# Scaled relus of ten tiles on VectorE, gates of three blocks by copies and gathers, one first load from ScalarE's queue, and a new order, in a gated linear-attention block

## The chip, the cores and the metric

The kernel runs on one core of a Trainium2 chip. The metric is the device time of one execution in microseconds (us), the median of several runs. In the profile PE is TensorE, ACT is ScalarE, DVE is VectorE, POOL is GpSimd, SP is SyncE, whose queue issues most of the DMAs; PEld is the loading of weights into TensorE.

## The reference

All data is float32: `x` is 2048 rows (tokens) of 512, H = 32 heads of 16.

```python
xn = layernorm(x)
# A: linear attention
q, k, v = heads(xn @ wqkv)                       # wqkv: 512 x 1536
phi = lambda t: where(t > 0, t + 1, exp(t)) + 1e-6
kv  = phi(k)^T v  per head;   z = sum over tokens of phi(k)
s   = (phi(q) kv) / (phi(q) . z + 1e-6) @ wo
# B: token mixing by shifts, then an MLP
h  = gelu(layernorm(xn) @ w1)                    # quarters shifted by +1, -1, +2, -2 tokens
x1 = xn + shifted(h) @ w2
y  = x1 + gelu(layernorm(x1) @ w3) @ w4          # w3: 512 x 1376
out = x + s * silu(y)
```

## The kernel before

**Tiles and stages.** The tokens are 16 tiles of 128 rows (`i` = 0 to 15), four tiles (`QT`) to a block `b` (0 to 3). Float32 accuracy is made of pairs: an operand is split into a rounded part and the rest (`hi`, `lo`), and a product is three matmuls (`products`). Products of 512 columns write a whole PSUM bank; there are four banks for running results ("mm") and four for long sums ("acc").

The first half of the program goes over the blocks. `load_u(b)` brings the block's transposed input `xt` and splits it into `u` (`ut` and `UT` in the code), `load_rows` brings `x` by rows and takes mean and variance: by two passes of ScalarE (tile `sq`) in block 0, by VectorE's statistics later; `scale_x` turns the variance into 1/sqrt on GpSimd (`rs`, `ns`, `nm`) and normalises the rows (`x`, `xh`, `xl`). For each tile there are then:

- `key(i)`: 12 matmuls into bank `k`; `feature_k` makes phi of it. `kt` = bank minus mean times column sum (VectorE), `kr` = relu(rs * kt) and then `kt` = exp(rs * kt) (ScalarE), `kr` = min(kt, 1) + kr (VectorE), then the halves `kh` and `kl`; a gather adds `kr` into `zacc`.
- `query(i)`: 12 matmuls into bank `q`; `qt` on VectorE, `qe` = relu(-rs * qt) and `qr` = relu(rs * qt) on ScalarE in another order of columns, `qe` = exp(-qe); `qr` is stored to memory and `qe` added there by a gather.
- `gram(i)`: 12 matmuls of `kh`, `kl` with `xh`, `xl` into the four long sums `g`.

`qneg` and `wneg` are the negated column sums of the weights; they come from one fp32 product each (`qsum`, `ksum`) with the sum of the four weight chunks (`wqt`, `wkt`). In the same half `mixer(b)` and `mix2(i)` do the token mixing (banks `h`, `pbm`, `pam`, `pem`). Between the halves `kv` and `m` join values and `wo`.

The second half goes over the blocks again. `up_last` (bank `a`) and five `up_pair`s (banks `pb`, `pa`, `pe`, a seven-product scheme, `seven`) make the MLP's hidden rows with gelu (`f`, `gf`); `down` adds their products with `w4` into the block's four accumulators (`acc`); `attend_pair` (banks `pbs`, `pas`, `pes`) makes `so`, the attention's output. In `seven` the bank `pb` is read by `p1` and `u2` on ScalarE and the bank `pe` by `p5`, before the next products go on top of them. `gate(i, a)` ends a tile: x1 is added to the accumulator, then tanh, two multiplications with `so`, a gather that adds `x`, and the store. The argument `late` chooses how x1 (kept in memory, `x1d`) is added: with it, x1 is fetched ahead and VectorE adds the accumulator; without it, ScalarE copies the accumulator and a gather of GpSimd adds x1 in SBUF. All calls of `before` use `late=True`. Blocks 0 to 2 call `gate` four times in a row; the last block has a code path of its own.

**The order.** The code above only records operations (`Plan.add`). `Plan.emit` then places them, engine by engine: it gives each a due time worked back from the order of TensorE's matmuls, keeps its own estimates of durations and of when an engine, a buffer or a DMA queue is free, and always takes the operation that can start first, by due time among those that can start within `slack`. TensorE may run ahead of its recorded order (`window`, `ahead`). Constants steer it: `PATIENCE` (how long a PSUM result may wait), `SAFE` (spare time behind a DMA), `lead` (how early buffers of a kind may be taken), and the table `SOONER`: pairs of an operation's number and how much earlier (in quarters of a us) it is due. The resulting order is fixed in the program; each engine works through its own list in order, and waits on semaphores.

`Plan.load` can issue a load from SP's queue or, with `eng="ACT"`, from ScalarE's; in `before` every load goes to SP. The first loads are the two halves of chunk 0 of block 0's `xt` (in `load_u`, parts > 1), and the key weights `wk_s`.

Of the kernel before, what the change touches and what calls it, by code (L numbers as in the profile page):

```python
# [10 lines left out]
AF = mybir.ActivationFunctionType  # L11
ALU = mybir.AluOpType
# [73 lines left out]
class Plan:  # L86
# [138 lines left out]


    GAP = .06
    PATIENCE = 2.5
    COLD, COLD_TILL = 1.84, 5.8
    SAFE = 2.0  # L230
    early = 0.0
    patience = 18.0

# [33 lines left out]
    def emit(self, first, lead, reserve, window, ahead, table=()):  # L267
# [20 lines left out]
        while left:  # L288
# [5 lines left out]
            for e, cands in avail.items():  # L294
                picks = []
                low = INF
                for op in cands:
                    s = max(free[e], op.ready)
                    if op.mb:
                        s = max(s, under[e == "POOL"][0] + self.GAP)  # L300
                    if op.two and s < port:
                        s = port
                    if e == "POOL" and not op.mb and not op.two:
                        s = next((b + .02 for a, b in lock if a <= s < b), s)
                    if op.table is not None and op.table != table:
                        s = max(s, free[e] + 1.28)
                    ok = True
                    fresh = [t for t in op.tiles if t.ap is None]
                    for t in fresh:
                        if t.tag not in slots:  # L310
                            continue
                        q = slots[t.tag]
                        need = sum(1 for u in fresh if u.tag == t.tag)
                        if len(q) < need:
                            ok = False
                            break
                        s = max(s, q[need - 1][0] + self.GAP)
                        if e == "PE":
                            if op is not front and (len(q) < 2 or op.nom - front.nom > ahead):
                                ok = False  # L320
                                break
                        elif t.tag in lead:
                            n = lead[t.tag] * (1.5 if len(q) > reserve[t.tag] else 1)
                            s = max(s, op.due + slip - n - t.early)
                    if not ok:
                        continue
                    if e == "PE" and op.nom - front.nom > window:
                        continue
                    q = s
                    if op.table is not None and op.table != table and op.due + slip < s:  # L330
                        q = s - 1.28
                    picks.append((q, s, op))
                    low = min(low, q)
                if not picks:
                    continue
                slack = .02 if e == "PE" else 0.08
                s, op = min(((s, op) for q, s, op in picks if q <= low + slack), key=lambda x: (x[1].due, x[1].order))
                if best is None or s < best[0]:
                    best = (s, op)
# [3 lines left out]
            e = op.eng  # L343
# [50 lines left out]
def linear_attn_gated_by_mixer(  # L394
# [20 lines left out]
    QT = 4  # L415
# [112 lines left out]
    def col(t, i):  # L528
        return t[:, i:i + 1]
# [105 lines left out]
    def load_u(b, parts):  # L635
# [3 lines left out]
        for q in range(parts):  # L639
            o = q * n  # L640
            for c in range(NC):
# [5 lines left out]
                        rounded(*(t[:, 2:2 + BT] for t in UT[b][c]), XT[b, c])  # L647
                    continue
                src = XT[b, c].cols(o, o + n)
                pl.load(src, xt[b, c][:, o:o + n])  # L650
                hi, lo = (t[:, 2 + o:2 + o + n] for t in UT[b][c])
                if b == q == 0 and parts > 1:
                    pl.ts(hi, src, 1.0, None, ALU.mult)
# [41 lines left out]
    def by_block(v):  # L695

        return v.via(lambda ap: ap.rearrange("p (b c k) -> p c b k", b=P // RB, k=RB))
# [41 lines left out]
    def feature_k(i, ps):  # L739

        t, r = piece(f"kt{i}"), piece(f"kr{i}")
        pl.stt(t, wneg, mean(mv1, i), ps, ALU.mult, ALU.add)
        pl.act(r, t, AF.Relu, scale=col(rs1, i))
        pl.act(t, t, AF.Exp, scale=col(rs1, i))
        hi, lo = rounds(f"k{i}")
        pl.stt(r, t, 1.0, r, ALU.min, ALU.add)
# [18 lines left out]
    def query(i):  # L765
# [2 lines left out]
        t, e, r = (piece(f"q{n}{i}") for n in "ter")  # L768
        pl.stt(t, qneg, mean(mv1, i), ps, ALU.mult, ALU.add)
        pl.act(by_block(e), by_chunk(t), AF.Relu, scale=col(ns1, i))  # L770
        pl.act(by_block(r), by_chunk(t), AF.Relu, scale=col(rs1, i))
        pl.act(e, e, AF.Exp, scale=-1.0)
        pl.soon(pl.store(pqd[i].all, r))
        pl.soon(pl.gather(pqd[i].all, e))
# [559 lines left out]
    for b in range(NQ):  # L1334
# [39 lines left out]
        if not last:  # L1374
# [2 lines left out]
                for j in range(QT):  # L1377
                    down(b, f, j, A[j])
            for j in range(QT):
                gate(b * QT + j, A[j], late=True)  # L1380
        else:
            i, (a, o) = b * QT + QT - 1, B[-1]
            XL[i] = piece(f"xo{i}")
# [15 lines left out]
                gate(b * QT + QT - 1, a, o, D // 2, late=True, by_dma=False, whole=o > 0)  # L1399

    SOONER = (
# [6 lines left out]
    )  # L1408
    pl.emit(first=6.0, lead={"p": 14.0, "w": 14.0, "ab": 10.0}, reserve={"p": 20, "w": 1, "ab": 0}, window=12.0,
            ahead=6.0, table=SOONER)  # L1410


# [35 lines left out]
```

## Time and profile before

| | |
|---|---|
| median of 3 runs | 519.17 us (518.96 to 519.18) |
| the profiled execution | 519.35 us, its span 517.6 us |
| PE busy | 511.2 us (99%), 3005 matmuls |
| DVE busy | 394.0 us (76%) |
| ACT busy | 324.8 us (63%) |
| POOL busy | 102.8 us (20%) |
| granted TensorE clock | 0.998 |

The span runs from the first instruction of the program to the last; the time has 1.75 us more around it. Busy time of PE is a union of modelled matmul spans that overlap, so a matmul that starts a little late need not show as idle time; the distance from one start to the next does show it. In rows of a timeline the columns are: start, duration, engine, line, operation, output and inputs (numbers left out), count, and in brackets the idle time of the engine ahead of it with what ended it. In rows of the chain: start, duration, what. In rows of a table by stretches: the stretch, its length, then busy us and instructions (x) of PE, PEld, DVE, ACT, POOL, then granted clock, DMA share and GB/s. In rows of groups: busy us, mean ns of one, and idle time before them.

### The profile page before, as it was taken

How to read it: one execution, taken by the hardware profiler on the slowest of the kernel's cores; microseconds unless marked ns; L12 is line 12 of the kernel's file. 1: busy time of each engine (PE TensorE's matmuls, PEld its weight loads, DVE VectorE, ACT ScalarE, POOL GpSimd, SP SyncE). 2: the span in 40 equal slices, each digit the busy share in tenths (PEclk: the TensorE clock that was granted, in tenths of full speed). 3: DMA queues.
4: the chain of work that ended last, by engine and by line, in shares of the span. 5: the costliest groups of instructions: out<-in, count | busy, mean ns of one | idle time of the engine just before them, and what ended most of it. 6: DMA issues, size and time to landing. Idle time of an engine off the chain costs nothing.

```text
span 517.6 us, 8927 instructions
## 1 busy us (share of the span) xinstructions
PE 511.2 (99%) x3005; PEld 445.0 (86%) x3005; DVE 394.0 (76%) x788; ACT 324.8 (63%) x664; POOL 102.8 (20%) x195
## 2 busy tenths in 40 slices
PE   8999999999999999999999999999999999999996
PEld 6777888988888888898889989899898898999985
DVE  5884987569567838999999999655886657895635
ACT  5899784579558657787866755345453545535621
POOL 1378643431363022211100001000020000200000
PEclk9999999999999999999999999999999999999999
DMA  8759994375976389989767759648488376687604
GB/s 277 255 101 248 225 205 97 74 172 182 220 169 162 68 185 249 259 261 262 287 200 225 237 175 249 212 152 208 133 214 276 122 201 157 179 248 225 243 1 122
DMA packets 73281, 100.12 MB, mean 193 GB/s; under 512 B 7844, under 2 KB 30900, under 8 KB 73236
## 3 DMA queue, kind: packets, MB, share of 16 engines
q1 hardware_dynamic: 63876, 82.52, 50.6%
q0 software_dynamic: 9360, 17.04, 19.9%
q8 instruction: 23, 0.38, 0.3%
q14 instruction: 22, 0.18, 0.1%
HBM read 60.33 MB, written 30.81 MB: 176 GB/s over the span
## 4 chain that ended last, share of the span: by engine, by line
PE 91%; ACT 5%; DVE 2%; DMA 1%; issue 1%; SPq 0%; DVEq 0%
PE acc L146 22%; PE pb L146 10%; PE k L146 8%; PE h L146 8%; PE q L146 7%; PE g L146 7%; PE pe L146 5%; PE pbs L146 5%; PE pbm L146 4%; PE pa L146 3%; PE pes L146 2%; PE a L146 2%; PE pem L146 2%; PE pas L146 1%; ACT y L167 1%; PE pam L146 1%
## 5 line engine op out<-in xcount | busy, mean ns | idle before, releaser
L223 POOL DMA_DIRECT2D th<-in_x x14 | 12.2, 919 | 247.3 <-PE a L146 126.2
L167 ACT ACTIVATE p<-pb 128x256 f32<-128x256 f32 x20 | 7.7, 385 | 25.8 <-PE pb L146 25.4
L223 POOL DMA_DIRECT2D o<-x x16 | 15.0, 935 | 40.4 <-DVE o L189 19.7
L223 POOL DMA_DIRECT2D zacc<-kr x16 | 14.6, 910 | 41.8 <-DVE kr L199 33.6
L167 ACT ACTIVATE th<-xo 128x512 f32<-128x512 f32 (+1 forms) x16 | 9.7, 619 | 19.3 <-DVE xo L189 16.2
L167 ACT ACTIVATE gf<-gf 128x512 f32<-128x512 f32 (+1 forms) x40 | 20.9, 523 | 0.8
L223 POOL DMA_DIRECT2D pqd<-qe x16 | 14.7, 921 | 28.9 <-ACT p5m L167 10.0
L167 ACT ACTIVATE p<-pe 128x256 f32<-128x256 f32 x20 | 7.7, 386 | 18.9 <-PE pe L146 18.9
L189 DVE TENSOR_TENSOR xo<-acc,xo 128x512 f32<-128x512 f32 (+1 forms) x16 | 10.3, 670 | 11.4 <-PE acc L146 11.4
L199 DVE SCALAR_TENSOR_TENSOR kt<-wneg,mv,k 128x512 f32<-128x512 f32 x16 | 11.9, 742 | 9.4 <-PE k L146 8.5
L199 DVE SCALAR_TENSOR_TENSOR kr<-kt,kr 128x512 f32<-128x512 f32 x16 | 11.0, 690 | 10.4 <-ACT kt L167 10.4
L199 DVE SCALAR_TENSOR_TENSOR qt<-qneg,mv,q 128x512 f32<-128x512 f32 x16 | 11.9, 742 | 7.2 <-PE q L146 7.1
L167 ACT ACTIVATE ht<-ht 128x512 f32<-128x512 f32 x16 | 10.0, 630 | 11.5 <-DVE ht L189 11.4
L189 DVE TENSOR_TENSOR gf<-u,pe 128x256 f32<-128x256 f32 x20 | 8.3, 416 | 11.2 <-PE pe L146 11.2
L189 DVE TENSOR_TENSOR gf<-pa,p 128x256 f32<-128x256 f32 x20 | 8.4, 418 | 10.5 <-PE pa L146 10.4
L189 DVE TENSOR_TENSOR ht<-h,abc 128x512 f32<-128x512 f32 x16 | 10.8, 686 | 6.5 <-PE h L146 6.5
L167 ACT ACTIVATE x<-x,nm,rs 128x512 f32<-128x512 f32 x16 | 12.5, 802 | 2.9 <-POOL nm L189 2.9
L167 ACT ACTIVATE qr<-qt,rs 128x512 f32<-128x512 f32 x16 | 11.4, 715 | 4.1 <-DVE qt L199 4.1
L590 DVE BATCH_NORM_STATS2 st<-o 128x6 f32<-128x512 f32 x16 | 10.9, 683 | 1.8 <-DMA o<-x 1.8
L167 ACT ACTIVATE kr<-kt,rs 128x512 f32<-128x512 f32 x16 | 11.4, 715 | 1.2 <-DVE kt L199 1.1
L167 ACT ACTIVATE y<-o,nm,rs 128x512 f32<-128x512 f32 x16 | 12.0, 805 | 0.1
L167 ACT ACTIVATE kt<-kt,rs 128x512 f32<-128x512 f32 x16 | 11.4, 715 | 0.1
(1559 smaller groups left out, 2195.9 us busy)
## 6 DMA issues: line engine op xcount, KB each, us to landing
w_s<-in_w SPq DMA_DIRECT2D x28, 256.0 KB, 5.5
x<-in_x SPq DMA_DIRECT2D x16, 256.0 KB, 5.2
zacc<-kr POOLq DMA_DIRECT2D x16, 256.0 KB, 3.9
pqd<-qr SPq DMA_DIRECT2D x16, 256.0 KB, 3.3
pqd<-qe POOLq DMA_DIRECT2D x16, 256.0 KB, 5.4
o<-x POOLq DMA_DIRECT2D x16, 256.0 KB, 4.6
x1d<-o SPq DMA_DIRECT2D x16, 256.0 KB, 4.9
pq<-pqd SPq DMA_DIRECT2D x16, 256.0 KB, 6.0
```

The costliest lines, as they stand in the source:

```text
L146: lambda: nc.tensor.matmul(out.get(), lhs.get(), rhs.get(), start=start, stop=stop, skip_group_check=more))
L167: nc.scalar.activation(out.get(), src.get(), func, scale=get(scale), **kw)
L189: self.vec(eng, out, [a, b], lambda: self.e(eng).tensor_tensor(out.get(), a.get(), b.get(), op=op), True)
L199: lambda: self.nc.vector.scalar_tensor_tensor(out.get(), a.get(), get(s), b.get(), op0=op0, op1=op1),
L223: lambda: self.nc.gpsimd.dma_start(out.get(), get(src), accum_op=ALU.add), mb=mb)
L590: pl.add("DVE", .62, .69, [xv], [st], lambda: nc.vector.bn_stats(st.get(), xv.get()))
```

## The change

Four things change, and the order of all engines with them.

1. The first half of `xt` (block 0, chunk 0) is issued by ScalarE's queue, so SP begins with the first key weight.
2. In `feature_k` the scaled relu of tiles 4 to 7 is one operation of VectorE (multiply by `rs`, then max with 0) instead of one of ScalarE; in `query` the same holds for `qr` of tiles 2 to 7. That is ten operations.
3. The gates of blocks 0 to 2 are called without `late`: ScalarE copies the accumulator, and a gather adds x1.
4. The planner's constants and its table are new.

```diff
-    PATIENCE = 2.5
+    PATIENCE = 6.0
...
-    SAFE = 2.0
+    SAFE = 1.5
...
-                slack = .02 if e == "PE" else 0.08
+                slack = .02 if e == "PE" else 0.15
...
-                pl.load(src, xt[b, c][:, o:o + n])
+                pl.load(src, xt[b, c][:, o:o + n], "ACT" if b == q == 0 and parts > 1 else "SP")
...
-        pl.act(r, t, AF.Relu, scale=col(rs1, i))
+        if QT <= i < 2 * QT:
+            pl.ts(r, t, col(rs1, i), 0.0, ALU.mult, ALU.max)
+        else:
+            pl.act(r, t, AF.Relu, scale=col(rs1, i))
...
-        pl.act(by_block(r), by_chunk(t), AF.Relu, scale=col(rs1, i))
+        if 2 <= i < 2 * QT:
+            pl.ts(by_block(r), by_chunk(t), col(rs1, i), 0.0, ALU.mult, ALU.max)
+        else:
+            pl.act(by_block(r), by_chunk(t), AF.Relu, scale=col(rs1, i))
...
             for j in range(QT):
-                gate(b * QT + j, A[j], late=True)
+                gate(b * QT + j, A[j])
...
-        19, 20867, 20, 10505, 21, 8920, 22, 8153, 23, 20874, 26, 12597, 28, 17, 29, 8881, 34, 1005, 35, 11144,
...
+        19, 21023, 20, 10241, 21, 8854, 22, 8160, 26, 12109, 29, 8773, 31, 300, 34, 620, 35, 17351, 42, 1204,
...
-    pl.emit(first=6.0, lead={"p": 14.0, "w": 14.0, "ab": 10.0}, reserve={"p": 20, "w": 1, "ab": 0}, window=12.0,
+    pl.emit(first=6.0, lead={"p": 12.0, "w": 20.0, "ab": 10.0}, reserve={"p": 20, "w": 1, "ab": 0}, window=12.0,
```

What the new order is in a few places: SP's first issue is `wk_s`; TensorE's list from the end of the first keys on is `qsum`, then query and gram of tiles 0, 1, 2, 3 by turns, twelve matmuls each, where before it was ten products of query 0, `qsum`, the rest of query 0, gram 0, query 1, four products of query 2, gram 1, the rest of query 2, gram 2, query 3, gram 3; ScalarE splits the `xt` of block 1 behind `k3h`, where before three of the four splits stood ahead of `kr` of tile 1; ScalarE does `zb` behind `u2m` of the last token mixing, where before it stood ahead of `p5m`; and the four sums `w_sf` of the second weight pair stand on VectorE's list ahead of the last `ht`, where before they stood behind it. The last block's list is nearly as before on every engine.

10 rows, old and new, of the table SOONER are left out of this document.

## The prediction

> **What bounds the kernel now.** I read the page first, then the chain of waits in order of time, then the timelines of the engines at the places where that chain leaves TensorE.
>
> ```profile
> span 517.6 us, 8927 instructions
> PE 511.2 (99%) x3005; PEld 445.0 (86%) x3005; DVE 394.0 (76%) x788; ACT 324.8 (63%) x664; POOL 102.8 (20%) x195
> ```
>
> TensorE (PE) is busy 99% of the span, and the change neither adds nor removes a matmul. So only three things can move the time: when PE starts its first real matmul, how often it starts one late, and the tail. The chain shows the front:
>
> ```profile
> 0.79 0.39 SPq L205
> ...
> 1.23 3.90 DMA wk_s<-in_wqkv
> ...
> 5.27 9.56 PE k L146 x34
> 14.83 0.87 PE ksum L146 x2
> ...
> 42.60 2.78 PE k L146 x12
> ```
>
> SP issues the first half of `xt` at 0.79 and the first key weight after it, at 1.23; that weight lands 3.90 us later, and PE starts `k` at 5.27. Twelve 128x512 products cost 2.78 us, an fp32 column sum 0.87. Now the same engine's own rows:
>
> ```profile
> 7.30 0.80 PE L146 MATMUL k<-wk_0h,u_0h 128*128 128x512 f32 x1
> ...
> 18.30 0.39 PE L146 MATMUL q<-wq_0h,u_0h 128*128 128x512 f32 x1
> ...
> 28.54 0.40 PE L146 MATMUL q<-wq_1h,u_1h 128*128 128x512 f32 x1
> 29.03 0.73 PE L146 MATMUL g<-k1h,x1h 128*128 128x512 f32 x2
> ```
>
> Between 18.30 and 42.60 PE does four query groups, four gram groups and `qsum`: 8 x 2.78 + 0.87 = 23.11 us of work in 24.30. So 1.19 us are lost there although the busy share reads full, because ends are modelled; starts tell. One visible piece: a 128x512 product takes 2.78 / 12 = 0.23, but from 28.54 to 29.03 are 0.49, so the gram of tile 1 came 0.26 late. The reason is ScalarE (ACT):
>
> ```profile
> 5.16 0.42 ACT L167 ACTIVATE wk_0h<-wk_s 128x256 fp32r<-128x256 f32 x1 [2.56 <-DMA wk_s<-in_wqkv]
> ...
> 15.73 0.60 ACT L167 ACTIVATE wneg<-ksum 128x512 f32<-128x512 f32 x1 [1.58 <-PE ksum L146]
> ...
> 17.36 0.71 ACT L167 ACTIVATE kr<-kt,rs 128x512 f32<-128x512 f32 x1
> ...
> 22.36 0.58 ACT L167 ACTIVATE qneg<-qsum 128x512 f32<-128x512 f32 x1
> 22.84 0.62 ACT L167 ACTIVATE u_2h<-xt 128x512 fp32r<-128x512 f32 x1
> ...
> 24.40 0.71 ACT L167 ACTIVATE kr<-kt,rs 128x512 f32<-128x512 f32 x1
> 25.02 0.71 ACT L167 ACTIVATE sq<-x,sx 128x512 f32<-128x512 f32 x1
> ...
> 27.04 0.80 ACT L167 ACTIVATE x<-x,nm,rs 128x512 f32<-128x512 f32 x1
> 27.75 0.71 ACT L167 ACTIVATE k1h<-kr,tiny 128x512 fp32r<-128x512 f32 x1
> 28.36 0.61 ACT L167 ACTIVATE x1h<-x 128x512 fp32r<-128x512 f32 x1
> ```
>
> From 16 us on ACT has no gap, and `x1h` goes at 28.36, just ahead of the late gram. From start to start a scaled relu or exp costs 0.62, a squared sum 0.70, a normalisation 0.71, `k1h` 0.61, `qneg` 0.48, and the three halves of the next block's `xt` between 22.84 and 24.40 cost 0.52 each: 1.56 us that nobody needs before the keys of tile 4, which PE starts at 42.60.
>
> **The change, part by part.** *The first loads.* The weight becomes SP's first issue, at 0.79 instead of 1.23, and the half of `xt` is issued by ACT at the same time; every later load of SP moves up one slot. ACT's table load goes behind that issue, which costs nothing: ACT stands idle 2.56 us before 5.16. If the weight takes its 3.90 us as now, PE starts 0.44 earlier; if the two loads share what the engines move, nothing is won. Nor is the whole of an earlier start kept: from 5.27 to 7.30 the four fp32 passes of the first two keys take 2.03, where `ksum`'s two take 0.87, so 1.74 for four; PE is still slow for 0.29 of it, and an earlier start lengthens the slow part. I take half, -0.2 (bounds 0 and -0.44).
> The Trainium skill ("DMA: Bandwidth & Descriptors", Issuing engines are not separate DMA queues) says that loads of different engines run on the same 16 DMA engines and interleave, so that a second issuer saves issue time only; by it the gain could not pass the slot of 0.44, and 0 is as good. The skill ("TensorE: Matmul & The Clock Gate", What's actually happening) gives half clock until about 3.4 us of sustained work; by it the earlier 0.44 is worth 0.22.
>
> *The front, 18 to 43 us.* In the changed kernel's own order PE has `qsum` ahead of the first query, and then q0, g0, q1, g1, q2, g2, q3, g3 without a break, where now g1 is pushed behind four products of q2. `qsum` ahead needs the third sum of the query weights one place earlier on VectorE (DVE):
>
> ```profile
> 2.97 0.30 DVE L194 TENSOR_SCALAR u_0h<-xt 128x256 fp32r<-128x256 f32 x1 [2.97 <-DMA xt<-in_xt]
> ...
> 16.36 0.75 DVE L199 SCALAR_TENSOR_TENSOR kt<-wneg,mv,k 128x512 f32<-128x512 f32 x1 [0.72 <-ACT wneg L167]
> ...
> 19.94 0.69 DVE L189 TENSOR_TENSOR wqt<-wqt,wq_s 128x512 f32<-128x512 f32 x1
> ```
>
> That 0.69 fits the idle 0.72 before `kt`. On ACT one more squared sum goes ahead of `wneg`, into its idle 1.58. So `kr` of tile 0 starts about 17.36 as now. From there ACT has, up to `k1h`: four relus and exps (2.48), two normalisations (1.42), two `xh` (1.04), two `kh` (1.22), four squared sums (2.80) and `qneg` (0.48): 9.44, so `k1h` is done at 26.8, 2.1 us before `x1h` ends now, because the three halves of `xt` stand behind tile 3 and two sums less stand between. `k1l` takes DVE another 0.69: 27.5. PE wants g1 at 18.30 + 0.87 + 3 x 2.78 = 27.5 and `k1l` 0.23 later: just in time. Tile 2 needs five more steps of ACT (3.1 us) and a DVE step, so about 30.6, against 27.5 + 2 x 2.78 = 33.1: no wait. So nearly all of the 1.19 goes; I take -1.0, bounds -0.4 (one of the tight places misses) and -1.19.
>
> *Ten relus to DVE.* Keys of tiles 4 to 7, queries of 2 to 7: ACT loses 10 x 0.62 = 6.2 us. The nearest rows for DVE are the one-input 128x256 above (0.30) and the two-input 128x512 (0.69), so 0.3 to 0.7 each; I take 0.45, being one-input: 4.5 us, at most 7.
>
> ```profile
> 35.00:40.00 5.00, 5.00 (x23) 4.05 (x22) 2.62 (x8) 5.00 (x10) 3.63 (x7) 1.00 0.76 141
> 40.00:45.00 5.00, 5.00 (x24) 4.02 (x23) 1.28 (x2) 5.00 (x10) 4.23 (x11) 1.00 0.89 220
> 45.00:50.00 5.00, 5.00 (x24) 3.93 (x23) 3.16 (x5) 4.48 (x9) 4.49 (x15) 1.00 1.09 289
> 50.00:60.00 10.00, 10.00 (x44) 8.08 (x44) 8.32 (x14) 9.17 (x17) 8.96 (x19) 1.00 0.90 222
> ```
>
> The third column of busy times is DVE, the fourth ACT: DVE is idle 2.38 + 3.72 + 1.84 + 1.68 = 9.6 us here and takes them in; nothing of PE's waits here. I cost it at 0; without that cover it would be their 4.5.
>
> *The stretch of 210 to 310 us.* DVE is nearly full here, and PE starts late twice:
>
> ```profile
> sum 100.00, PE 99.65 PEld 89.41 DVE 98.68 ACT 73.84 POOL 8.36; mean PE 9.96 PEld 8.94 DVE 9.87 ACT 7.38 POOL 0.84
> ```
> ```profile
> 221.59 0.28 PE L146 MATMUL pbm<-w_t2h,hs23l 128*128 128x256 f32 x1
> 222.15 0.38 PE L146 MATMUL pem<-w_b22h,hs43h 128*128 128x256 f32 x1 [0.28 <-ACT p5m L167]
> ...
> 262.83 0.40 PE L146 MATMUL acc<-w_1l,f_1h 128*128 128x512 f32 x1
> 263.30 0.39 PE L146 MATMUL pb<-yt40h,w_b 128*128 128x256 f32 x1
> ```
> ```profile
> 220.73 0.58 ACT zb L167
> ...
> 253.94 0.42 DVE L189 TENSOR_TENSOR w_sf<-w_s,w_s 128x256 f32<-128x256 f32 x1
> ```
>
> With 0.12 for a 128x256 product the first costs 0.56 - 0.12 = 0.44, the second 0.47 - 0.23 = 0.24. In the new order ACT does `zb` (0.58) after `p5m`, but two more copies for `w3` (2 x 0.52) ahead of the last `ht`, where it idles about 0.7 now: net some 0.3 earlier. DVE has four `w_sf` sums (4 x 0.42 at most) done before the last `ht`, but three small steps more between the two `gf` that decide at 263. I take half of the 0.68 away, -0.35, bounds +0.4 and -0.7.
>
> *Gates of blocks 0 to 2.*
>
> ```profile
> 303.55 2.52 DVE L189 TENSOR_TENSOR xo<-acc,xo 128x512 f32<-128x512 f32 x4
> ```
> ```profile
> L167 ACT ACTIVATE gs<-g 128x512 f32<-128x512 f32 x4 | 2.4, 589 | 0.0
> ```
> ```profile
> th<-in_x POOLq DMA_DIRECT2D x14, 256.0 KB, 6.0
> ```
> ```profile
> DMA to landing us min/median/max: 1.7/5.7/7.7
> 311.07 0.39 ACT L167 ACTIVATE u<-pb 128x256 f32<-128x256 f32 x1 [0.33 <-PE pb L146]
> ```
>
> DVE loses 12 sums (four take 2.52), ACT gains 12 copies out of PSUM (0.59, like `gs`), SP loses 12 fetches, GpSimd gains 12 accumulating gathers. The accumulators come free as early as now. But the tanh now waits for its gather, and behind it in ACT's queue stand the gelus and the copies of `pb` and `pe` for the next pair, for which PE waits. The new order puts the first tanh of block 0 behind `u` (311.07 now). Its copy can go about 303.6, so it is done at 304.2; a gather that lands in the 6.0 us of the gates' other gathers is there at 310.2, covered by 0.9 (the row with 7.7 as the longest is for all transfers of `th`, stores too). Cost 0; the last block's gates and the tail are as before.
>
> **Sum.** -0.2 - 1.0 - 0.35 = -1.55. The profiled execution took 519.35 (1.75 around its span), which gives 517.8; the median of the runs is 0.18 lower, so 517.6.
>
> **Rivals.** *Given back by DVE.* DVE's 98.68 of 100 us leaves no room: if PE comes 1.2 us earlier to it and DVE cannot, the gain ends there, 517.6 + 1.2 = 518.8. For it: that share. Against it: the stretch hangs on PE's last `h` products, and moves forward with them. 14%. *The front is not met.* `k1l` has no slack by my count; if ACT or a load lags by a microsecond, the 1.0 stays lost, and with the +0.4 of the stretch: 519.17 - 0.2 + 0.4 = 519.4. 8%. *Slower, by the gathers of the gates.* Four accumulating gathers go out close together at each of three block ends. Up to 6.9 us to landing they are hidden; at 9 (7.7 is the longest row) the head of ACT's queue stands 2.1 us, and PE, which has a dozen products of the next accumulators (2.78 / 12 each) to put before the next `pb`, loses about 1 of it at each end: 3 in all, so 517.6 + 3 = 520.6. For it: nothing else in ACT's queue there waits on a transfer now. Against it: the median row is 6.0. 12%.
>
> **Chances.** Forecast as worked out 66%. About 0.2% (1.04 us) can be told from no change here. Faster by more: the forecast's 66%. Within: the first two rivals, 22%. Slower: 12%. The likeliest case alone runs from 516.8 (all bounds good: -0.44 - 1.19 - 0.7) to 518.1. The range reaches up over the two middle rivals, 519.5, and leaves out the third.
>
> **What would show it.** Right: `k` starts near 5.0, the fourth key group (42.60 now) near 41.4, no start-to-start gap before g1 and g2, and at 222 and 263 at most half of the gaps. Wrong: PE waiting for `kr`, `k1l` or `qsum`'s sum before 30 us; new gaps before `pb` between 230 and 300; ACT idle on a DMA before `th` near 311, 380 or 450 with PE's `pb` late behind it.

## The result and the profile after

The changed kernel takes 521.70 us (median of 6 runs, 520.97 to 522.94), the kernel before 519.33 beside it: ratio 1.0046, interval 1.0035 to 1.0057. It is slower by 2.4 us; 517.6 was forecast. A second set of runs of the same kernel gave 521.17 and a ratio of 1.0041 (1.0027 to 1.0054). The profiled execution of the first set is its fastest run (520.97, span 519.0).

The head of its page, which answers to the two lines of before:

```profile
span 519.0 us, 8890 instructions
PE 512.3 (99%) x3005; PEld 445.2 (86%) x3005; DVE 392.4 (76%) x786; ACT 328.2 (63%) x666; POOL 112.7 (22%) x207
```

It says next to nothing: a busy share of 99% both times. What tells is where the same matmul starts in both executions. In the following table each number is the median, over the matmuls that start within 2.5 us of the time at the head of the column in the kernel before, of start in the named execution minus start in the execution of before (us; negative: PE is ahead). A step from column to column is a gain or loss in between. The names are those of the experiments below.

```
              15     40     65     80    100    150    200    250    300    400    500
after       -0.23  -0.72  -0.69  -0.18   0.25   0.40   0.59   0.47   1.00   1.01   1.04
after_again -0.30  -0.20  -0.16   0.34   0.78   0.93   1.09   1.00   1.51   1.54   1.21
a_relu_act  -0.27  -0.39  -0.36   0.17   0.29   0.47   0.67   0.63   1.16   1.09   1.66
a_loads2    -0.51  -0.69  -0.61  -0.67  -0.54   0.17   0.34   0.22   0.77   0.71   0.77
b_relu_dve  -0.44  -0.44  -0.44   0.19   0.16   0.16   0.20   0.52   0.73   0.80   0.80
h_midA      -0.38  -0.39  -0.39  -0.39  -0.42  -0.32  -0.13  -0.19   0.37   0.42   0.51
b_gather     0.44   0.43   0.43   0.43   0.42   0.39   0.41   0.39   0.38   0.07   0.28
h_best4     -0.47  -1.06  -0.97  -0.98  -1.00  -1.03  -1.03  -1.11  -1.02  -1.01  -0.96
```

The row of after: 0.72 ahead by 40 us, all of it and 0.25 more lost between 65 and 100 in two steps, then 0.75 more lost from 100 to 300, and nearly nothing from there to the last matmul, which starts 1.09 late. The profiled execution is longer by 1.62 (520.97 for 519.35): 0.27 more come between the start of the last matmul and the end of the span (5.07 us for 4.80), and 0.26 outside the span. The prediction took the tail as unchanged; what makes it longer was not tried. The column of 15 shows how much the start alone differs from run to run.

The first step is at 73 us. TensorE and VectorE there, after, and the `k7l` of before:

```profile
72.99 0.40 PE L146 MATMUL g<-k7h,x7h 128*128 128x512 f32 x1
73.70 0.50 PE L146 MATMUL g<-k7l,x7h 128*128 128x512 f32 x1 [0.31 <-DVE k7l L199]
```
```profile
72.36 0.69 DVE L189 TENSOR_TENSOR w_b22l<-w_s,w_b22h 128x512 fp32r<-128x512 f32 x1
72.96 0.69 DVE L199 SCALAR_TENSOR_TENSOR k7l<-kr,k7h 128x512 fp32r<-128x512 f32 x1
```
```profile
73.28 0.69 DVE L199 SCALAR_TENSOR_TENSOR k7l<-kr,k7h 128x512 fp32r<-128x512 f32 x1 [0.20 <-ACT k7h L167]
```

From 72.99 to 73.70 are 0.71 where 0.23 is the step. VectorE delivers `k7l` 0.32 earlier than before, but PE is 0.7 earlier: the stall is the lead that VectorE could not follow. The table of stretches, before and then after, shows why (third busy time is DVE, fourth ACT):

```profile
60.00:75.00 15.00, 15.00 (x66) 12.11 (x65) 14.34 (x24) 11.59 (x20) 5.11 (x9) 1.00 0.95 211
```
```profile
60.00:75.00 15.00, 14.69 (x64) 11.61 (x63) 14.96 (x27) 8.09 (x14) 3.84 (x6) 1.00 0.75 159
```

VectorE had 0.66 us free in 15 and has 0.04; ScalarE went from 3.4 idle to 6.9. And VectorE comes to this stretch late, for a reason on SP's queue. SP's issues before and after, then VectorE at 57 us after, and the row of the chain that it goes back to:

```profile
29.61 7.07 SPq L210 DMA_DIRECT2D pqd<-qr  x2
36.78 2.41 SPq L205 DMA_DIRECT2D w_s<-in_w  x4
39.28 3.27 SPq L210 DMA_DIRECT2D pqd<-qr  x2
42.65 2.77 SPq L205 DMA_DIRECT2D w_s<-in_w  x4
```
```profile
31.15 9.85 SPq L210 DMA_DIRECT2D pqd<-qr  x4
41.05 2.34 SPq L205 DMA_DIRECT2D w_s<-in_w  x4
...
46.07 2.61 SPq L205 DMA_DIRECT2D w_s<-in_w  x4
```
```profile
56.98 0.69 DVE L189 TENSOR_TENSOR w_f<-w_s,w_s 128x512 f32<-128x512 f32 x1 [1.23 <-DMA w_s<-in_w]
```
```profile
46.77 10.11 DMA w_s<-in_w
```

The stores of the query relus stand ahead of the loads of the mixing weights: four of them in a row where there were two, and SP stands 9.85 us at them, because they wait for their `qr` (the second and the last go at 36.49 and 40.68, just behind the `qr` that end at 36.47 and 40.65). So `w1` is issued 4.3 us later and the second set 3.4 us later; a weight of that set lands at 56.9, VectorE idles 1.23 for it and then has the same work in less time.

### The profile page after: what moved, and what is told of

Read it like the earlier page. It is cut to its first block, busy times and chain, and to the rows that moved or that the text cites. A ratio compares the mean times of both kernels' runs of the same rounds, so it can differ in the third digit from the quotient of the medians.

```text
span 519.0 us, 8890 instructions
## 1 busy us (share of the span) xinstructions
PE 512.3 (99%) x3005; PEld 445.2 (86%) x3005; DVE 392.4 (76%) x786; ACT 328.2 (63%) x666; POOL 112.7 (22%) x207
## 4 chain that ended last, share of the span: by engine, by line
PE 83%; ACT 8%; DVE 6%; DMA 2%; issue 1%; SPq 0%; POOL 0%; DVEq 0%; ACTq 0%; POOLq 0%
PE acc L146 23%; PE pb L146 11%; PE h L146 6%; PE k L146 6%; PE pe L146 6%; PE pbs L146 5%; PE q L146 4%; PE pbm L146 4%; PE g L146 4%; PE pa L146 3%; PE pes L146 2%; PE a L146 2%; PE pem L146 2%; DMA w_s<-in_w 2%; ACT x L167 1%; PE pas L146 1%
## 5 line engine op out<-in xcount | busy, mean ns | idle before, releaser
L223 POOL DMA_DIRECT2D xo<-x1d x12 | 10.6, 1128 | 167.5 <-ACT xo L167 107.3
L223 POOL DMA_DIRECT2D o<-x x16 | 13.9, 871 | 43.9 <-DVE o L189 36.9
L199 DVE SCALAR_TENSOR_TENSOR qz<-pq,zb 128x512 f32<-128x512 f32 x16 | 10.6, 681 | 2.6 <-PE acc L146 2.6
L199 DVE SCALAR_TENSOR_TENSOR th<-th,so 128x512 f32<-128x512 f32 (+1 forms) x17 | 11.2, 656 | 1.4
```

What stands on the lines that cost most here:

```text
L199: lambda: self.nc.vector.scalar_tensor_tensor(out.get(), a.get(), get(s), b.get(), op0=op0, op1=op1),
L223: lambda: self.nc.gpsimd.dma_start(out.get(), get(src), accum_op=ALU.add), mb=mb)
```

## The experiments

In the experiments marked "order kept" the planner runs to its end first, with the kernel's own engines and costs, and gives the order; then the operations are emitted in it, with an edit. So one part can be undone without a new plan for all others. The code shown in this section is shortened, with names in place of the operations' numbers.

```diff
-            op.emit()
+            seq.append((op, new))
...
+        for op, new in edit(seq):
+            ...
+            op.emit()
```

Times are medians beside the kernel before on the same chip.

**The relus.** a_relu_act: changed kernel, order kept, and in each of the ten places

```diff
-    nc.vector.tensor_scalar(r, t, rs, 0.0, mult, max)
+    nc.scalar.activation(r, t, Relu, scale=rs)
```

> The changed kernel with its order kept fixed on every queue; the ten scaled relus alone are issued by ScalarE again, each at the place in the sequence where VectorE had it. Relu theory (VectorE, without a gap from 57 to 73 us, is late with k7l because three of the ten relus, 0.40 each from start to start, stand ahead of it there): the 0.58 lost at 73 us goes, the 0.32 at 93 us goes at least in part, and the time is 0.6 to 0.9 below the changed kernel's 521.7, so 520.8 to 521.1. Order theory (the second weight set's products, put ahead of the keys of tile 7 on VectorE, make it late): ScalarE had 3.3 us of idle time there, k7l comes earlier by what the relus took, but the other losses, at 93 and from 222 to 300, stay; 521.1 to 521.5. Gates theory (the gathers of the gates cost the time and the spread of the runs): no change, 521.5 to 521.9. The price the other way: ScalarE takes 6.2 us back, and if it is the bound between 26 and 43 us the time gets longer by up to 1.

520.83, ratio 1.0026 (1.0013 to 1.0039): 0.9 below the first runs of the changed kernel and 0.3 below the second, as the relu theory said or less, and not by its way. (The profiled execution, 521.55, is the longest of its six, so its row in the table ends higher than the median.) The loss at 93 us is gone (0.17 at 80, 0.29 at 100); the one at 73 is all there. VectorE, then SP's queue:

```profile
59.35 0.69 DVE L189 TENSOR_TENSOR w_f<-w_s,w_f 128x512 f32<-128x512 f32 x1 [0.62 <-DMA w_s<-in_w]
...
73.29 0.69 DVE L199 SCALAR_TENSOR_TENSOR k7l<-kr,k7h 128x512 fp32r<-128x512 f32 x1
```
```profile
31.49 12.11 SPq L210 DMA_DIRECT2D pqd<-qr  x4
43.68 3.35 SPq L205 DMA_DIRECT2D w_s<-in_w  x4
```

VectorE, freed of three relus, waits for the late weights instead, and these are later than in the changed kernel: SP now stands 12.11 us at the four stores and issues `w1` at 43.68 for 41.05. So it is not the relus' move to VectorE that makes the weights late but the place of the four stores on SP's list; the move brings their `qr` earlier. b_relu_dve is the other side, the relus alone on VectorE in the order of before:

> The kernel before with its order kept fixed on every queue; the ten scaled relus alone are issued by VectorE, each at the place in the sequence where ScalarE had it. Prediction's view (VectorE takes ten relus of 0.4 in for nothing): 519.2 to 519.5. Relu theory (VectorE is full from 60 to 73 us and again to 93; three relus ahead of k7l, five ahead of hs40l): PE waits at 73 or at 93 us, 0.3 to 0.9 in all: 519.6 to 520.2.

520.35 against 519.11, ratio 1.0025 (1.0009 to 1.0041): slower. 0.63 of it lies at 73 us, where the weights are early and four of the relus stand between 60 us and `k7l`:

```profile
70.27 0.48 DVE L750 TENSOR_SCALAR kr<-kt,rs 128x512 f32<-128x512 f32 x1
...
73.52 0.69 DVE L199 SCALAR_TENSOR_TENSOR k7l<-kr,k7h 128x512 fp32r<-128x512 f32 x1
```

Most of the other 0.6 arises between 225 and 300, where no relu stands; I did not find out why.

**The weight loads.** a_k7 moves three operations of VectorE (order kept):

```diff
+    MOVED = ((w_2l, behind kr7), (w_f, behind kr7's sum), (w_b22l, behind k7l))
```

> The changed kernel with three operations of VectorE moved a little: the low part of one half of w1 (w_2l) behind the relu of key 7, one weight sum (w_f) behind the sum of key 7, and w_b22l behind k7l. Nothing is added or taken away. If these three, 0.6 each, standing ahead of key 7 are what makes k7l late, the 0.58 at 73 us goes and k7l is ready by 72.9. If nothing later takes it back, 521.1; if VectorE is the bound again at 82 to 93 us whatever happens at 73, PE loses the same 0.58 there and the time stays at 521.7.

521.42, no gain: the wait is only moved. ScalarE, then VectorE:

```profile
71.97 0.63 ACT L167 ACTIVATE w_t3h<-w_f 128x512 fp32r<-128x512 f32 x1 [1.74 <-DVE w_f L189]
72.51 0.71 ACT L167 ACTIVATE k7h<-kr,tiny 128x512 fp32r<-128x512 f32 x1
```
```profile
73.25 0.69 DVE L199 SCALAR_TENSOR_TENSOR k7l<-kr,k7h 128x512 fp32r<-128x512 f32 x1 [0.71 <-ACT k7h L167]
```

`w_t3h` stands ahead of `k7h` on ScalarE and waits for the `w_f` that I had put off. a_loads2 goes to the root, on SP's queue:

```diff
-    pqd2, pqd3 (stores), w1 x4 (loads), arow0 (store), w2 x4 (loads)
+    w1 x4 (loads), pqd2, pqd3 (stores), w2 x4 (loads), arow0 (store)
```

> The run a_loads again with other buffers: that kernel gave tiles the buffer that was freed first by the place in the listing, this one gives the buffer that is freed first by the planner's times, as the changed kernel does. Eight loads moved up on SP's queue, nothing else. Queue theory: no wait for k7l at 73 us, and PE ahead of the kernel before by 0.3 to 0.7 at 75 to 90 us; what PE loses at 93 us for hs40l (0.32 in the changed kernel) stays or goes with it. If the stall at 145 us and the one at 402 in a_loads came from the buffers, they are gone, and the median is 521.0 to 521.4. If the early loads themselves cost it, it stays at 522.5.

520.68, ratio 1.0023 (1.0007 to 1.0039), 1.0 less than the changed kernel's first runs, and 0.5 less than its second. With all ten relus on VectorE the loss at 73 is gone, and most of that at 93 with it (-0.61, -0.67, -0.54 in the table). So in the changed order the wait at 73 hangs on the late weights and not on the relus. That the same relus cost 0.63 there in the order of before fits the lists: before has `w_f`, `w_t3l` and `w_t4l` ahead of `k7l` on VectorE, the changed order has them behind it. SP, then VectorE:

```profile
36.90 2.86 SPq L205 DMA_DIRECT2D w_s<-in_w  x4
...
41.33 3.84 SPq L205 DMA_DIRECT2D w_s<-in_w  x4
```
```profile
55.72 0.68 DVE L189 TENSOR_TENSOR w_f<-w_s,w_s 128x512 f32<-128x512 f32 x1
...
71.97 0.68 DVE L199 SCALAR_TENSOR_TENSOR k7l<-kr,k7h 128x512 fp32r<-128x512 f32 x1
```

But at 127 us PE then loses 0.7 at once, behind the copy `p1m` of ScalarE: the lead meets the next place that has no slack for it.

**Four kernels with badly chosen buffers.** a_loads (the same loads), h_endB, h_frontA and h_best1 were written from lists, with each new tile in the buffer freed first by place in the list.

> The changed kernel, nothing but eight loads moved up on SP's queue: the four of the first mixing weights (w1) ahead of the stores of the relus of queries 2 and 3, the four of the second set (w2) ahead of the store of the row arow. In the changed order SP stands 9.85 us at four stores of query relus from 31.15 on and issues the weights at 41.05 and 46.07, where before it did so at 36.78 and 42.65. Queue theory: the late weights leave VectorE idle before 57 and make it late with k7l and hs40l; with the loads early the waits at 73 us (0.58) and 93 us (0.32) go, PE is still 0.7 us ahead of the kernel before at 75 to 90 us, and the time is 520.8 in the median. Relu theory: the three relus ahead of k7l are the cause, and both waits stay within 0.1 of what they were, at 521.7.

> The changed kernel up to 298 us in the changed order, and from there in the order of the kernel before (at this place both orders have done the same operations, so one can go over into the other); gates by fetch and VectorE sum throughout, for the order before needs them so. End theory: in the changed order the turned queries of the last pair of tiles (q14t) are loaded 7 us later than before, just when they are needed, and their landing sets the spread of the runs and the last 0.7 of the time; with the end in the order before, the runs lie within 0.8 us of each other and the median is 520.3 to 520.6, that is, 519.2 plus the 1.0 that PE has lost by 300 us. Rival (the end costs nothing in the median, all is lost by 300 and by the noise of the machine): 521.2 to 521.7.

> The changed kernel up to 96 us (first loads, ten relus on VectorE, changed order), from there the order of the kernel before, gates as before. By the traces PE is then 0.2 us behind the kernel before at 96 us and stays so: 519.3 to 519.6, not to be told from the kernel before. If the stretch from 96 to 300 costs time whatever its order is, because VectorE is full there, it would be 520 or more.

> An attempt at a version ahead of both: first half of xt by ScalarE's queue and the changed order up to 55 us, with the relus of queries 2 to 5 and keys 4 and 5 on VectorE and the weight loads early as in the kernel before; from 55 us on the order of the kernel before, with its relus on ScalarE, and gates as before. If the 0.7 us that PE gains by 43 us is kept where nothing of the old order waits, 518.4 to 518.7. If VectorE, which has 10.00 of 10 us at 60 to 70 in the kernel before, cannot come earlier, it is lost between 60 and 95: 519.1 to 519.4.

522.48, 525.57, 525.13 and 525.78. The three that end in the order of before all stall near 391 us. TensorE of h_endB, and what VectorE waits for there:

```profile
391.63 0.39 PE L146 MATMUL acc<-w_0h,f_0h 128*128 128x512 f32 x1
395.36 0.58 PE L146 MATMUL pb<-yt42h,w_b 128*128 128x256 f32 x1 [3.34 <-DVE gf L189]
```
```profile
DVE qz L199 <- DMA out<-th: 3.7, 1, 3.7
```

`qz` had been given a buffer that a store of `out` was still reading, and everything behind it on VectorE stood. (The expectation of h_endB2 below calls it a wait for a PSUM bank; that was my misreading.) The stall costs more than itself, since TensorE comes out of it at half clock. The granted clock (third number from the end) of h_endB:

```profile
394.60:401.40 6.80, 6.04 (x17) 5.08 (x18) 3.78 (x7) 2.45 (x6) 0.00 (x0) 0.50 0.60 190
```

A 128x512 product takes 0.43 there for 0.23, and of the 6.2 us that h_endB loses between 300 and 400 the wait itself is 3.5. In h_frontA a wait of 2.59 us is followed by 3.4 us at half clock. These times say nothing of the change, only that the choice of buffer is part of the order. The later lists take buffers by the planner's times.

**Which stretch.** At 96 us and at 298 us both orders have done the same operations, so one can go over into the other. h_frontA2 has the changed kernel's first 96 us, h_midA only its order from 96 to 298, h_endB2 all but the end:

```diff
+    h_frontA2: after[:96 us] + before[96 us:]
+    h_midA:    before[:96 us] + after[96 us:298 us] + before[298 us:]
+    h_endB2:   after[:298 us] + before[298 us:]
```

> The changed kernel up to 96 us (first loads, ten relus on VectorE, changed order), from there the order of the kernel before with its gates; buffers by the planner's times. At this place both orders have done the same operations. Front theory (late weights and relus on VectorE take the 0.7 gained by 43 us away again at 73 and 93 us and leave PE 0.1 to 0.3 behind): 519.2 to 519.5, no more, so the rest of the loss lies behind 96 us. Rival (all of the loss starts in the front and only shows later): 520.5 or more.

> The kernel before (its first loads, relus and gates), with the changed order from 96 us to 298 us alone. Middle theory (in every kernel with this order PE lost 0.8 to 0.9 between 100 and 300 us against the kernel before, whatever the relus, loads and gates were): 519.8 to 520.1. Rival (the order there is as good, and the losses are those of a disturbed front): 519.0 to 519.3.

> The run h_endB again with buffers given by the planner's times, since the one wait of 3.5 us at 391 us there, which was the same in all kernels with listed buffers, was for a PSUM bank. The changed kernel up to 298 us, from there the order of the kernel before; gates by fetch and VectorE sum. End theory (the late load of the turned queries of the last pair sets the spread and the last part of the loss): runs within 0.8 us of each other, median 520.2 to 520.6. Rival (no cost in the end, all lost by 300 us): 521.2 to 521.7 with a spread as the changed kernel's.

h_frontA2: 520.07, ratio 1.0017 (1.0005 to 1.0029), more than expected: the front costs not 0.2 but 0.5 (trace, from 15 to 100 us) to 0.9 (times). h_midA: 520.14, ratio 1.0016 (1.0004 to 1.0028): at the upper end of what was expected, with the 0.8 in the table between 100 and 300. h_endB2: 521.29, ratio 1.0043 (1.0029 to 1.0056), inside the rival's range: the end costs nothing that shows. Its five runs lie within 0.8, but those of a_loads2 (eight, within 0.84) and of after_again (five, within 0.62), which have the changed end, lie no further apart. So the spread of the first six runs says nothing of the end.

a_none undoes all three edits of the source and keeps the order:

> The changed kernel's order (fixed up to about 295 us) with none of the three changes of the source: first half of xt issued by SP, relus on ScalarE, gates by fetch and VectorE sum. What is left is the order alone. If the order alone loses, it stays at 521 or above. If the relus and the gates lose and the order is good, it comes to 519 to 520.2 (plus 0.2 for the first loads).

520.86, ratio 1.0028 (1.0017 to 1.0039), between the two expectations: the order alone costs 1.6 of the 2.0 to 2.4, though it was planned for relus on VectorE and may suit ScalarE's worse. This kernel comes to 73 us without a lead (0.09 behind) and loses nothing there. It loses 0.5 ahead of 40 us, where `g1` waits, and 0.9 between 100 and 300.

**The gates.** a_late and b_gather switch them each way; the plan is the same up to 295 us.

```diff
-    gate(b * QT + j, A[j])
+    gate(b * QT + j, A[j], late=True)
```

> The changed kernel with the gates of blocks 0 to 2 by fetch and VectorE sum as before; all else as changed, and every queue's order is the same up to about 295 us. Gates theory: the time falls to 520.8 to 521.0 and the runs lie within 0.8 us of each other instead of 2. Relu and order theories: 521.4 to 521.9 in the median, since in the profiled run the gates cost 0.3 at most (a late start at 332 us and one at 390).

> The kernel before with the gates of blocks 0 to 2 by ScalarE copies and gathers, nothing else; the order is the same up to about 295 us. Gates theory (they cost nothing, as predicted; putting fetch and sum back into the changed kernel moved it by 0.4 at most): 518.9 to 519.4. The slower rival of the prediction (gathers land late, and ScalarE's queue holds the gelus back): 520 or more, with PE late before pb near 311, 380 or 450 us.

521.68 (changed order, fetch and sum) and 519.45 (order before, gathers; ratio 1.0006, 0.9994 to 1.0018): no difference that can be told. In b_gather the gathers take to landing what the prediction took, and the first tanh stands ahead of `u`, which is then at 311.47 for 311.07 before, no later than this execution is at 300 anyway (0.38):

```profile
xo<-x1d POOLq DMA_DIRECT2D x12, 256.0 KB, 6.1
```
```profile
303.70 0.60 ACT L167 ACTIVATE xo<-acc 128x512 f32<-128x512 f32 x1 [0.81 <-PE acc L146]
...
310.95 0.62 ACT L167 ACTIVATE th<-xo 128x512 f32<-128x512 f32 x1
311.47 0.38 ACT L167 ACTIVATE u<-pb 128x256 f32<-128x256 f32 x1
```

**A version ahead of both.** h_best2 takes the changed order only up to 50 us, with the weight loads early, and the order, relus and gates of before from there; relus on VectorE where it has room (keys 1 and 4, queries 2 to 4). The first half of `xt` is issued by ScalarE. h_best3 adds two edits, h_best4 only the second of them:

```diff
+    kr of i in (1, 4), qr of 2 <= i < 5 on VectorE; after[:50 us] + before[50 us:]
...
-    "ACT" if b == q == 0 and parts > 1 else "SP"     (h_best3 only)
+    "SP"
...
-    zb, hs43h, p5m, gs, u2m     (ScalarE, h_best3 and h_best4)
+    hs43h, p5m, gs, u2m, zb
```

> An attempt ahead of both: first half of xt by ScalarE's queue; the changed order up to 50 us, with the eight weight loads early as in the kernel before, relus of keys 1 and 4 and of queries 2 to 4 on VectorE; from 50 us on the order of the kernel before with relus on ScalarE and gates as before. The relu of key 1 on VectorE takes 0.6 off ScalarE ahead of k1h, so g1 should come without its wait at 27 us (0.5 in the changed kernel) and PE should be 1.0 to 1.2 ahead of the kernel before at 50 us. If that is kept: 518.0 to 518.4. If VectorE or ScalarE cannot come earlier between 57 and 95: 518.9 to 519.4.

> The kernel h_best2 with two edits: the first half of xt is issued by SP again, and the copy zb of ScalarE stands behind u2m instead of ahead of p5m. First loads: in the profiles with ScalarE's queue the half of xt lands at 4.5 to 5.6 us and the first k starts at 4.8 to 5.7, with SP's it lands at 3.0 and k starts at 5.2 to 5.3 behind the weight; so it costs nothing to put it back, or gains up to 0.1. zb: p5m can go when pem is done, at about 220.5 instead of 221.0, and the stall of 0.45 + 0.1 ahead of pem near 221 us goes to below 0.15. In all 518.0 to 518.3. If the stall at 221 comes from hs43h or its low part and not from p5m, it stays, and the time is 518.4 to 518.7. If ScalarE's queue for the first load was worth 0.2, that is 0.2 more.

> The kernel h_best2 with zb of ScalarE behind u2m instead of ahead of p5m, nothing else. In h_best3 that took 0.22 off at 221 us and PE gave 0.17 of it back by 231 (pbm waits there instead). So: 518.4 to 518.6, no difference to h_best2's 518.56, if the 0.6 that h_best3 was slower came from the first load on SP; 519.0 to 519.3 if moving zb costs it.

h_best2: 518.56, ratio 0.9986 (0.9977 to 0.9994). h_best3: 519.19. h_best4: 518.45, ratio 0.9984 (0.9975 to 0.9993), the fastest here, 0.75 below the kernel before. The lead of 1.06 at 40 us is still 0.96 at 500; 0.47 of it is there at 15 us already, which is the start of this execution and not the order. Ahead of g1 one more relu off ScalarE takes nearly all of the wait away; TensorE of after and of h_best4:

```profile
27.29 0.42 PE L146 MATMUL g<-k1h,x1h 128*128 128x512 f32 x1
27.94 0.50 PE L146 MATMUL g<-k1l,x1h 128*128 128x512 f32 x1 [0.23 <-DVE k1l L199]
```
```profile
27.23 0.40 PE L146 MATMUL g<-k1h,x1h 128*128 128x512 f32 x1
27.60 0.50 PE L146 MATMUL g<-k1l,x1h 128*128 128x512 f32 x1
```

The first loads of h_best3 and h_best4 differ and nothing else, so by the medians ScalarE's first issue is worth 0.7 in this order; in the changed order a_none (SP's) and a_relu_act (ScalarE's), which differ in the gates too, are the same (520.86, 520.83). How far the start of a single execution can move by itself stands in the last section. after_again, the changed kernel a second time, was run for the start:

> The changed kernel unchanged. If the early start of its first profile belongs to the change, k starts at 4.8 again; if it was luck of that run, at 5.1 to 5.7 as in the kernels with the same first loads, and PE is behind the kernel before by 0.2 to 0.5 more at the end than the 1.1 of the first profile. Waits at 73 us (k7l, 0.4 to 0.6) and 93 us (hs40l, 0.3) again. Time 521.2 to 522.0.

521.17; `k` at 5.05, between the two cases. The first `u_0h` of after, and the first `k` of after, of after_again and of h_best4:

```profile
4.49 0.29 DVE L194 TENSOR_SCALAR u_0h<-xt 128x256 fp32r<-128x256 f32 x1 [4.49 <-DMA xt<-in_xt]
```
```profile
4.78 1.98 PE L146 MATMUL k<-wk_s,xt 128*128 128x512 f32 x2
```
```profile
5.05 1.19 PE L146 MATMUL k<-wk_s,xt 128*128 128x512 f32 x1
```
```profile
5.20 1.14 PE L146 MATMUL k<-wk_s,xt 128*128 128x512 f32 x2 [0.30 <-DMA xt<-in_xt]
```

Issued by ScalarE, the half of `xt` lands at 4.5 or later, where it landed at 2.97, close to the weight. In 12 of the 14 profiles with this issue it lands last, and PE waits for it instead of for the weight; in after and after_again the weight is still the later one, by 0.17.

## Why the prediction was wrong, point by point

**The steps that failed: a lead taken as kept, and the -0.35.** The sum has -1.2 for all that comes ahead of 96 us (first loads and front) and nothing for what the lead meets on its way; the kernel with that part alone, h_frontA2, is 0.9 slower than before. It has -0.35 for the stretch of 210 to 310; the order from 96 to 298 alone, h_midA, is 0.9 slower too. The order with none of the edits of the source (a_none) costs 1.6 where the sum has -1.35 for it (front and stretch). The prediction costed the places where TensorE was late before. It did not ask which operation just ahead of each product has no slack, once TensorE comes 0.7 earlier or the order is another: `k7l` at 73 us, `hs40l` at 93, and in the middle places that were not found one by one.

**The ten relus, 0.** "DVE is idle 2.38 + 3.72 + 1.84 + 1.68 = 9.6 us here and takes them in; nothing of PE's waits here". The size was right (0.40 from start to start, 0.45 taken). The cover was not shown: the rows ended at 60 us, and three of the ten, with the keys that PE waits for, stand between 60 and 73, where VectorE had 0.66 free in 15. In the order of before the ten cost 1.2 (b_relu_dve), 0.63 of it at 73 us. In the changed order they are not what makes the wait there: it stays without them (a_relu_act) and goes with them (a_loads2). The prediction put them at 4.5 without cover; in the order of before they cost a quarter of it.

**What it left out: SP's order.** It counted SP's fetches and its first slots, but did not follow the weight loads past the stores of `qr`. Putting them back is worth 0.5 to 1.0 (a_loads2). The relus are not behind it: with them on ScalarE the same stores hold the loads 2.6 us longer.

**The front, -1.0.** Half right. `qsum` ahead and the queries and grams by turns cost no wait; "`k1l` has no slack by my count" was the place that missed, by 0.5 in the first profile and by 0.9 in the second. Its lower bound of -0.4 held in the first; the fourth key group starts at 41.70, for 42.60 before and 41.4 forecast. What made `k1l` late is the sum of 9.44 for ScalarE: from `kr` of tile 0 to the end of the step of `k1h` it takes 9.94 (17.13 to 27.07 in after). The second half of it:

```profile
23.71 0.71 ACT L167 ACTIVATE kr<-kt,rs 128x512 f32<-128x512 f32 x1
24.45 0.72 ACT L167 ACTIVATE kt<-kt,rs 128x512 f32<-128x512 f32 x1
25.08 0.80 ACT L167 ACTIVATE x<-x,nm,rs 128x512 f32<-128x512 f32 x1
25.92 0.63 ACT L167 ACTIVATE x1h<-x 128x512 fp32r<-128x512 f32 x1
```

The relu takes 0.74 from start to start where 0.62 was counted, and the normalisation 0.84 where 0.71 was. The counted steps come from rows of before in which another tile's operation follows; here the next one takes the same tile. With one more relu off ScalarE the whole is there: h_best2 goes from 0.23 behind at 15 us to 0.77 ahead at 40, a gain of 1.0, and keeps it. So the term could be had, by one relu more; in the changed kernel half of it was missed here, and the rest was lost later.

**The stretch of 210 to 310, -0.35.** Wrong sign. The two stalls shrank by the half that was taken (0.31 for 0.44 at 222, and the one at 263 went), but new ones came, as at 250:

```profile
250.19 0.28 PE L146 MATMUL pb<-yt20h,w_s0l 128*128 128x256 f32 x1
250.47 0.38 PE L146 MATMUL pe<-yb220h,w_s1h 128*128 128x256 f32 x1
```

0.28 where 0.12 is the step. h_midA shows the whole stretch of that order at +0.8 without any edit of the source, in steps of 0.1 to 0.3 from 140 on; which operation makes each late was not tried. I had costed the two places that were late before and none of those that were not. The zb by itself is worth nothing: in h_best4 the stall at 221 shrinks by 0.2, and PE gives that back by 231.

**The first loads, -0.2.** Not shown. "`k` starts near 5.0" came true, but with the same first loads fourteen profiles have it at 4.78 to 5.65, and six with SP's issue at 5.15 to 5.47. The chain mostly waits for the other transfer now. Nor does an early start decide: after starts `k` at 4.78 and its product behind the four passes at 7.05, h_best4 at 5.20 and 6.64, since the full clock begins at 6.55 in the one and at 5.27 in the other (last section). In the kernel before it begins at 6.57, so PE was at half clock for 1.30 us from 5.27 on, which costs some 0.65 and not the 0.29 of the prediction. The Trainium skill ("DMA: Bandwidth & Descriptors", Issuing engines are not separate DMA queues) says that a second issuer saves issue time alone, and the prediction read from it that a gain of 0 was as good; the start of `k` agrees, while the 0.7 between the medians of h_best3 and h_best4 is more than the slot of 0.44, and stays open.

**The gates, 0.** Not contradicted, and with it the slower rival has the wrong cause: its "slower" came from the gathers, and they cost 0.2 by the medians, not clear of noise. By the trace of b_gather PE loses nothing between 300 and 500, and the end of the span behind the last matmul is 0.25 longer (5.05 for 4.80); a_late, without gathers, has 5.02 there, so that is not shown to be theirs either.

**The rivals.** "Given back by DVE" named the mechanism, but put it at 210 to 310; it acts at 73 and 93; at 127, with these mended, PE waits for a copy of ScalarE. The sum, from the medians of the kernels that hold one part each: up to 96 us 0.9, middle 0.9, gates 0.2, together 2.0 of the 2.0 to 2.4 measured. By the traces the first two are 0.5 and 0.8. Where the loss lies is shown by these kernels; for the wait at 73 us an edit shows the cause (the late weights), for the middle the operations stay open.

## What to carry to other kernels

Cover for a moved operation has to be read in the few microseconds ahead of the one product that waits for it, not as idle time summed over a stretch; a lead on the bounding engine is kept only if every helper on its way has slack for it. Follow the loads on a queue that is worked in its list's order past each store that waits for a computed tile: such a store holds back a weight that has nothing to do with it. And when a planner makes the order anew, keep the old order and apply the edits one by one: here the order alone cost more (1.6) than any edit alone (1.2), and the first 50 us of it, mended, ahead of the old order were better than either kernel.

## What the runs showed of the hardware

The first products are not always equally slow. TensorE of h_best3 and of h_midA, the same four fp32 passes and the two products behind them:

```profile
5.47 3.75 PE L146 MATMUL k<-wk_s,xt 128*128 128x512 f32 x4 [0.58 <-DMA wk_s<-in_wqkv]
8.23 1.42 PE L146 MATMUL k<-wk_0h,u_0h 128*128 128x512 f32 x1
9.45 0.61 PE L146 MATMUL k<-wk_0l,u_0h 128*128 128x512 f32 x1
```
```profile
5.30 1.95 PE L146 MATMUL k<-wk_s,xt 128*128 128x512 f32 x4 [0.40 <-DMA wk_s<-in_wqkv]
6.88 0.61 PE L146 MATMUL k<-wk_0h,u_0h 128*128 128x512 f32 x1
7.32 0.40 PE L146 MATMUL k<-wk_0l,u_0h 128*128 128x512 f32 x1
```

From the first start to that of the last row are 3.98 and 2.02. By `ksum` (0.87 for two passes) and a product of 0.23, full clock would need 1.97, and half clock 3.94. The clock records in the traces agree: their first stretch at full clock begins at 9.91 us in h_best3 and at 5.24 in h_midA. (The clock column of the tables by stretches reads 1.00 ahead of the first record too, and does not show it.) In all 20 profiles it begins between 4.04 and 7.34 us, but for h_best3 and h_frontA2 with 9.91 and 10.29; in these two `ksum` starts at 16.43 and 16.67, in the others at 14.09 to 15.11. That is most of the spread in the column of 15 of the table.

The profiled executions of these two are also well above the medians of their kernels (520.35 for 519.19, 521.96 for 520.07). The Trainium skill ("TensorE: Matmul & The Clock Gate", What's actually happening) says that the clock is released by a window of activity that runs freely, so that the place of the change differs from run to run; these rows and records agree. That this parts the executions that were not profiled, or makes the 0.7 between the medians of h_best3 and h_best4, is not shown.
